# Four small moves in the order of work of an attention-then-experts kernel on one core

## The chip, the cores and the metric

The kernel runs on one core of a Trainium2 chip. Its time is the device time in microseconds (us), the median of several runs. The engines of the core are named as in the profile: PE (TensorE matmul) and PEld (its weight loads), DVE (VectorE), ACT (ScalarE), POOL (GpSimd) and SP (SyncE, which here only issues DMAs). Matmuls and weight loads are in float32 for all that matters here; the trace shows each such matmul as two passes, so 4 matmuls are "x8".

## The reference, cut to what matters

Two blocks follow each other. The first is an attention without softmax, the second routes each row by a hash to one of eight experts.

```python
def _attn_ref(q, k, v, S1, S2):          # q, k, v: (4, 4, 1088, 32); S1, S2: (8, 32)
    def phi(x):                          # 64 features of a row
        a = np.einsum('rd,bhsd->bhsr', S1, x)
        b = np.einsum('rd,bhsd->bhsr', S2, x)
        return np.einsum('bhsi,bhsj->bhsij', a, b).reshape(*x.shape[:-1], r * r)
    q_p, k_p = (phi(q), phi(k))
    kv = np.einsum('bhsf,bhsd->bhfd', k_p, v)
    ...                                  # num = q_p @ kv, den = q_p @ sum(k_p)
    return (num / den).astype(np.float32)

def _moe_ref(x, token_ids, w1, w2):      # x: (4352, 128), w1: (8, 128, 1024), w2: (8, 1024, 128)
    expert_idx = token_ids * np.int64(2654435761) % np.int64(E)
    for e in range(E):
        xe = x[mask]                     # rows of expert e
        out[mask] = np.maximum(xe @ w1[e], 0.0) @ w2[e]
```

## The kernel before, in words

**Order.** The whole kernel stands in a hand-written schedule: every engine runs its instructions in the order in which the Python code records them. So where a line stands in the code decides what is queued behind it on its engine. Waits between engines are semaphores that a tile framework puts in, by regions of tiles.

**Loads.** SP issues all input loads at the start (L95 to L152), in this order: k of batch 0 in two halves, k of batch 1, q of batch 0 in two halves, v of batch 0 in two halves, then the tails (the last 64 of a batch's 1088 rows: two DMAs for k, two for v), q of batch 1, two DMAs for the tails of q, v of batch 1, and then batches 2 and 3 and the first expert weights. A tail tile holds two batches in partitions 0 to 63 and two in 64 to 127, and each DMA of `load_tail` (L102, issue at L106) fills one half. Completion semaphores of these DMAs are used in turn, eight of them, so a DMA's issue waits until the one eight places ahead has landed.

**Attention, batch by batch.** For k, PE transposes the rows (L421), ACT copies them out of PSUM (L429), PE multiplies with the sketch matrices (L455, tile `ab_ps`), ACT copies the result (L470), DVE multiplies the two sketches into features `kp` (L482, 1024 columns per half of a batch), and PE sums `kv` over the batch's rows (L513). The tail's features are `kp_tail` and its `kv` matmuls come last in each batch. For q, DVE transposes 32 by 32 blocks (`q_blocks`, L549; for batch 0 written out at L683, in halves), PE multiplies (L455, `abq_ps`), ACT copies, DVE makes features `f` (L482) and transposes them to `fT` (L565), and PE multiplies them with `m`, the block-diagonal copy of `kv` that ACT makes (L535), into `x_ps` (L617). The q tails go through `q_tail_blocks` (L573), L582, `q_tail_features` (L602, L605) and `x_tail_products` (L626). ACT copies `x_ps` to `xe` (L620, L629); `denominators` (L639, L640) and `x_main` (L645) with `x_tail` (L659) divide and write rows to a DRAM tensor `x_rows` (DMAs at L653 and L661). `x_main` runs on POOL for batches 0 and 1 and on DVE for batches 2 and 3.

**Prologue around the change.** Between the loads and the loop over batches the code (L666 to L709) builds the routing of tokens (DVE L291 to L318, PE L299, POOL `route_firsts`, `route_digits`, `route_slots`) among the first features of k and q. On DVE the order is: scan of the routing, `kp` first half, q's blocks of batch 0 in two halves, four routing steps, the sum of digits, `kp` second half, `f` and `fT` of the first half of q, q's blocks of batch 1, `kp_tail`, blocks of the q tail, and `f` and `fT` of the second half.

**Experts.** 16 groups of work follow (256 columns each for the first eight, 320 for the overflow eight). Group g does eight steps c: `layer1` (L891) and, for the group before, `layer2` (L899). The results of `layer1` are evicted by ACT for even c (L765) and by DVE for odd c (L767). In group 0 there is no `layer2` yet, so its steps are half as long. Other work is hung on a step by `at(g, c, f, ...)` and runs after that step's matmuls. Gathers of rows from `x_rows` (POOL indirect DMAs, L759) go ahead of the groups that need them, each with a small DVE copy of its index (L811); the tiles of the first eight groups read only rows of batches 0 and 1. `turn_in` and `join_in` (L830, L831, L836) transpose gathered rows by DMA, `bring` (L822) by PE. `rows_of` (tag `xs`) has one buffer, so the rows of batch 3 wait until the DMA has read those of batch 2.

Of the kernel before, what the change touches and what calls it, by code (L numbers as in the profile page):

```python
# [9 lines left out]
F32 = mybir.dt.float32  # L10
# [20 lines left out]
def kernel(  # L31
# [12 lines left out]
    nc = tc.nc  # L44
    P = 128
    B, H, S, D = q.shape
# [4 lines left out]
    T = S // P  # L51
    SM = T * P
    SP = S - SM
    TT = B // 2
    Q = P // D
# [19 lines left out]
    work = ctx.enter_context(tc.tile_pool(name="work", bufs=2))  # L75
# [23 lines left out]
    def tail_rows(b):  # L99
        return slice(b // TT * SP, (b // TT + 1) * SP)  # L100

    def load_tail(src, name):  # L102

        t = const.tile([P, TT, H, D], F32, name=name)
        for b in range(0, B, TT):
            nc.sync.dma_start(t[tail_rows(b)].rearrange("p t h d -> p (t h) d"),  # L106
                              src[b:b + TT, :, SM:, :].rearrange("t h p d -> p (t h) d"))
        return t

    def load_main(src, b, tag):  # L110
        t = load.tile([P, H, T, D], F32, tag=tag, name=f"{tag}{b}")
        n = parts(b, tag)
        for g in range(n):
            nc.sync.dma_start(t[:, :, g * T // n:(g + 1) * T // n],
                              src[b, :, g * SM // n:(g + 1) * SM // n, :].rearrange("h (p t) d -> p h t d", t=T // n))
        return t
# [5 lines left out]
    k_t, v_t, q_t = [], [], []  # L122
# [23 lines left out]
    k_tail = load_tail(k, "k_tail")  # L146
    v_tail = load_tail(v, "v_tail")
    q_t.append(load_main(q, 1, "q"))
    q_tail = load_tail(q, "q_tail")
    v_t.append(load_main(v, 1, "v"))  # L150
    for b in range(2, B):
        load_batch(b)  # L152
# [53 lines left out]
    GQ = T // Q  # L206
# [89 lines left out]
    def route_counts():  # L296
        cnt = bank([P, 3, E], "cnt")
        for n, w in enumerate((before, ones_h, early)):
            nc.tensor.matmul(cnt[:, n], w[:], cp[:], start=True, stop=True)  # L299
        counts = const.tile([P, 3, E], F32, name="counts")  # L300
        nc.scalar.copy(counts[:], cnt[:])
        return counts
# [4 lines left out]
    def route_bases(cnt):  # L307
        nc.vector.tensor_scalar(took[:], cnt[:, 2], float(GE), None, op0=OP.min)
        nc.vector.tensor_tensor(left[:], cnt[:, 1], took[:], op=OP.subtract)

        base = const.tile([P, E], F32, name="base")
        nc.vector.scalar_tensor_tensor(base[:], took[:], float(1 << RB), cnt[:, 0], op0=OP.mult, op1=OP.add)
        nc.vector.tensor_tensor(seq[:], seq[:], base[:].unsqueeze(2).to_broadcast([P, E, C]), op=OP.add)
# [21 lines left out]
    def route_firsts():  # L335

        nc.gpsimd.memset(late[:], 1.0)
        nc.gpsimd.tensor_scalar(first[:], eid[:], float(GE), -1.0, op0=OP.mult, op1=OP.add)
        nc.gpsimd.tensor_scalar(first_late[:], eid[:], float(GL - GE), float(E * GE), op0=OP.mult, op1=OP.add)
# [84 lines left out]
    def transposed(src, g):  # L424
        return kT_copied(turned(src, g))
# [32 lines left out]
    def k_products(kTs):  # L458

        ab_ps = bank([P, T // Q, H, Q, 2 * R], "ab_ps")  # L460
        for g, kT in enumerate(kTs):
            for h in range(H):
                wide_products(ab_ps[:, g, h:min(h + 2, H)], kT[:, h], s_k[:])
        return ab_ps

    def ab_tile():
        return work.tile([P, T, H, 2, R], F32, tag="ab", name="ab", bufs=3)

    def copy_ab(ab, ab_ps, g, src=None):
        nc.scalar.copy(ab[:, g:g + Q].rearrange("p t h x r -> p t h (x r)"),  # L470
                       ab_ps[:, g // Q if src is None else src].rearrange("p h t y -> p t h y"))

    def copied(ab_ps):

        ab = ab_tile()
        for g in range(0, T, Q):
            copy_ab(ab, ab_ps, g)
        return ab

    def features(dst, ab, eng=nc.vector):  # L480
        shape = list(dst.shape)
        eng.tensor_tensor(dst, ab[:, :, 0].unsqueeze(3).to_broadcast(shape),  # L482
                                ab[:, :, 1].unsqueeze(2).to_broadcast(shape), op=OP.mult)
# [8 lines left out]
    def k_features_of(kp, ab, lo, hi, eng=nc.vector):  # L492
        features(kp[:, lo:hi].rearrange("p t h i j -> p (t h) i j"), ab[:, lo:hi].rearrange("p t h x r -> p (t h) x r"), eng)

    def values(vsrc, n, pool, tag, copy=nc.gpsimd.tensor_copy):

        va = pool.tile([P, n, H, DA], F32, tag="va" + tag, name="va" + tag, bufs=1)
        nc.gpsimd.memset(va[:, :, :, D:DA], 1.0)
        if copy:
            copy(va[:, :, :, 0:D], vsrc[:].rearrange("p h t d -> p t h d"))  # L500
        return va
# [41 lines left out]
            nc.scalar.copy(m[r, :, h], kv[r, :, h * DA:(h + 1) * DA])  # L543
        return m

    def q_blocks(src, n):

        qT = work.tile([P, H, n, D], F32, tag=f"qT{n}", name="qT", bufs=1)
        nc.vector.transpose(qT[:].rearrange("p h t s -> p (h t s)"), src[:].rearrange("p h t d -> p (h t d)"))  # L549
        return qT  # L550

    def q_products(qT, n):
# [17 lines left out]
    def q_tail_blocks():  # L570

        qT = work.tile([P, TT, H, FB, D], F32, tag="xs", name="qT_tail", bufs=1)
        nc.vector.transpose(qT[:].rearrange("p t h k s -> p (t h) k s"),  # L573
                            q_tail[:].rearrange("p t h d -> p (t h) d").unsqueeze(2).to_broadcast([P, TT * H, FB, D]))
        return qT
# [93 lines left out]
    route_scan()  # L669
    va = values(v_t[0], T, work, "", None)  # L670
    route_firsts()
    abk = ab_tile()
    kp = work.tile([P, T, H, R, R], F32, tag="kp", name="kp", bufs=1)
    parts_ps = [k_products(kTs[g:g + 1]) for g in range(GQ)]
    copy_ab(abk, parts_ps[0], 0, src=0)
    nc.scalar.copy(cp[:], seq[:, :, C - 1])
    copy_ab(abk, parts_ps[1], Q, src=0)
    k_features_of(kp, abk, 0, Q)
    cnt = route_counts()
    kTs = [transposed(k_t[1], g) for g in range(0, T, Q)]  # L680
    qT = work.tile([P, H, T, D], F32, tag=f"qT{T}", name="qT", bufs=1)
    for g in range(GQ):
        nc.vector.transpose(qT[:, :, g * Q:(g + 1) * Q].rearrange("p h t s -> p h (t s)"),  # L683
                            q_t[0][:, :, g * Q:(g + 1) * Q].rearrange("p h t d -> p h (t d)"))
    route_bases(cnt)
    digits = route_ranks()
    k_features_of(kp, abk, Q, T)
# [2 lines left out]
    for g in range(GQ):  # L690
        ts = slice(g * Q, (g + 1) * Q)
# [11 lines left out]
    kv = kv_products(0, (kp, va), (kp_tail, va_tails), kv, T)  # L703
    abk = copied(abk_ps)
    fTs = [q_features(abq, 0)]
    qT = q_blocks(q_t[1], T)
    k_features_of(kp_tail, abt, 0, TT)
    qT_tail = q_tail_blocks()
    fTs.append(q_features(abq, 1))  # L709

    for b in range(EB):
        kv = kv_products(b, (kp, va), (kp_tail, va_tails), None if b else kv)
        if b > 0:
            abk_ps = k_products(kTs)
        abq_ps = q_products(qT, T)
        va = values(v_t[b + 1], T, work, "")
        if b == 0:
            route_slots()
        if b == 0:
            abt_ps = q_tail_products(qT_tail)  # L720
        m = kv_diagonal(b, kv)
        if b == 0:
            tail = q_tail_copied(abt_ps)
            kT_ps = [turned(k_t[b + 2], g) for g in range(0, T, Q)]
        else:
            abk = copied(abk_ps)
        kp = k_features(abk, T, work, "")
        if b == 0:
            fT_tail = q_tail_features(tail)

        x_products(b, 0, fTs[0], m)
        abq = copied(abq_ps)
        m_tail = kv_tail(b, kv)
        x_products(b, 1, fTs[1], m)
        x_tail_products(b, m_tail)
        qT = q_blocks(q_t[b + 2], T)
        if b == 0:
            kTs = [kT_copied(p) for p in kT_ps]
            fTs = [q_features(abq, 0)]
            route_rows(0)  # L740
            route_tiles()
        else:
            route_tiles_p()
            kTs = [transposed(k_t[b + 2], g) for g in range(0, T, Q)]
            route_rows(1)
        denominators(b, 0, GQ * HQ + H)
        for g in range(GQ):
            x_main(b, g, nc.gpsimd)
        x_tail(b, nc.gpsimd)
        if b == 0:  # L750
            load_experts(range(E // 2, E - 2))
        if b == 0:
            fTs.append(q_features(abq, 1))
        else:
            fTs = [q_features(abq, 0)]
# [83 lines left out]
    b, e = EB, EB + 1  # L839
# [7 lines left out]
    abk, abq = copied(abk_ps), copied(abq_ps)  # L847
# [4 lines left out]
    kp = k_features(abk, T, work, "")  # L852
# [151 lines left out]
    def at(g, c, f, *a):  # L1004
        beside.setdefault((g, c), []).append(lambda: f(*a))
# [10 lines left out]
            at(g, 1 + c, fetch_tile, *ahead.pop(0))  # L1016
    assert not ahead

    for g, c in zip(range(GQ), (1, 4)):
        at(0, c, x_main, e, g, nc.vector)  # L1020
    at(0, 5, x_tail, e, nc.vector)
    for k in range(11, G):
        for j in range(tiles_of(k)[1]):
            at(k - 3, 1 + j, fetch_tile, k, j)
# [28 lines left out]
    g, lo = G - 1, GL - P  # L1053
# [40 lines left out]
    with tc.For_i(0, turns):  # L1094
# [19 lines left out]
        at = moe.tile([P, C], F32, tag="at", name="at", bufs=1)  # L1114
# [70 lines left out]
```

## Time and profile before

| what | value |
|---|---|
| median of 5 runs | 196.41 us (195.55 to 197.03) |
| the profiled execution's own time | 195.88 us |
| its span, first to last instruction | 194.2 us |
| mean granted TensorE clock | 0.990 |
| PE, DVE, POOL, ACT busy | 185.3, 111.3, 103.1, 73.7 us |
| DMA moved | 26.09 MB, mean 134 GB/s |

The span is 1.7 us shorter than the execution's own time. Timeline rows have the start, the length, the engine, the line, the operation, the tiles and sizes, the number of instructions merged, and in brackets how long the engine had stood idle and what ended that. The view of stages has, for each stretch of time, the busy time of every engine with its number of instructions, then the granted clock, the share of the 16 DMA engines and GB/s. PE's busy time counts modelled ends of pipelined matmuls, so short gaps between matmuls do not show in it; they are found from the starts.

### The profile page before, as it was taken

How to read it: one execution, taken by the hardware profiler on the slowest of the kernel's cores; microseconds unless marked ns; L12 is line 12 of the kernel's file. 1: busy time of each engine (PE TensorE's matmuls, PEld its weight loads, DVE VectorE, ACT ScalarE, POOL GpSimd, SP SyncE). 2: the span in 40 equal slices, each digit the busy share in tenths (PEclk: the TensorE clock that was granted, in tenths of full speed). 3: DMA queues.
4: the chain of work that ended last, by engine and by line, in shares of the span. 5: the costliest groups of instructions: out<-in, count | busy, mean ns of one | idle time of the engine just before them, and what ended most of it. 6: DMA issues, size and time to landing. Idle time of an engine off the chain costs nothing. (4 is left out here: it accounts for less than half of the span.)

```text
span 194.2 us, 3346 instructions
## 1 busy us (share of the span) xinstructions
PE 185.3 (95%) x1064; PEld 155.7 (80%) x1064; DVE 111.3 (57%) x302; ACT 73.7 (38%) x227; POOL 103.1 (53%) x137
## 2 busy tenths in 40 slices
PE   7989999999999999999999999999999999999960
PEld 2889999999998888888888887777777777777960
DVE  5699999999968843454345344253446625232320
ACT  6552874758365323322332322223313231321220
POOL 7228982818464466466655744656465441434650
PEclk9999999999999999999999999999999999999995
DMA  4969999999379452333324324222243421300100
GB/s 130 292 128 271 351 359 340 341 363 334 102 192 316 138 125 68 71 81 80 85 67 102 79 68 93 56 68 71 68 93 65 92 70 27 66 14 25 48 27 9
DMA packets 40737, 26.09 MB, mean 134 GB/s; under 512 B 21785, under 2 KB 37916, under 8 KB 40720
## 3 DMA queue, kind: packets, MB, share of 16 engines
q1 hardware_dynamic: 35888, 19.15, 35.4%
q0 software_dynamic: 2304, 4.59, 8.9%
q10 hardware_dynamic: 2528, 2.13, 3.8%
q8 instruction: 9, 0.15, 0.3%
q14 instruction: 8, 0.07, 0.1%
HBM read 17.47 MB, written 4.59 MB: 114 GB/s over the span
## 5 line engine op out<-in xcount | busy, mean ns | idle before, releaser
L891 PE MATMUL hp<-xT,w 128*128 128x256 f32 (+3 forms) x272 | 81.8, 393 | 0.0
L899 PE MATMUL op<-hT,w 128*128 128x256 f32 (+2 forms) x256 | 79.0, 399 | 0.0
L767 DVE TENSOR_SCALAR hT<-hp 128x256 f32<-128x256 f32 (+3 forms) x68 | 29.8, 440 | 64.3 <-PE hp L891 61.4
L891 PEld LDWEIGHTS hp<-xT,w 128*128 128x128 f32 x272 | 50.1, 190 | 11.7 <-DVE hT L767 0.4
L902 POOL DMA_INDIRECT out_dram<-os,put x36 | 36.1, 1003 | 43.2 <-DVE os L955 27.6
L899 PEld LDWEIGHTS op<-hT,w 128*128 128x128 f32 x256 | 48.2, 190 | 12.8
L765 ACT ACTIVATE hT<-hp 128x256 f32<-128x256 f32 (+3 forms) x68 | 27.2, 400 | 66.9 <-PE hp L891 66.9
L759 POOL DMA_INDIRECT xg<-x_rows,idx x34 | 35.0, 1029 | 20.5 <-DVE idx L811 8.1
L617 PE MATMUL x_ps<-m,fT 128*128 128x132 f32 x128 | 15.7, 279 | 0.1
L513 PE MATMUL kv<-va,kp 128*128 128x132 f32 x128 | 15.6, 278 | 0.0
L617 PEld LDWEIGHTS x_ps<-m,fT 128*128 128x128 f32 x128 | 14.9, 190 | 0.4 <-ACT xe L620 0.3
L513 PEld LDWEIGHTS kv<-va,kp 128*128 128x128 f32 x128 | 14.9, 190 | 0.1
L934 ACT COPY half<-op 128x256 uint16<-128x256 uint16 (+1 forms) x26 | 8.8, 392 | 13.2 <-PE op L899 13.2
L535 ACT COPY m<-kv 32x66 f32<-32x66 f32 x48 | 9.9, 206 | 7.3 <-PE kv L513 6.7
L482 DVE TENSOR_TENSOR kp<-ab 128x1024 f32<-128x1024 f32 x8 | 11.1, 1414 | 0.8 <-ACT ab L470 0.8
L482 DVE TENSOR_TENSOR f<-ab 128x1024 f32<-128x1024 f32 x8 | 10.5, 1311 | 0.1
L565 DVE STREAM_TRANSPOSE fT<-f 128x1024 f32<-128x1024 f32 x8 | 10.0, 1246 | 0.5
L645 POOL TENSOR_TENSOR xs<-xe,den 128x512 f32<-128x512 f32 x4 | 4.9, 1243 | 8.6 <-DVE f L482 5.1
L455 PE MATMUL abq_ps<-s_k,qT 128*128 128x128 f32 (+1 forms) x64 | 7.8, 275 | 0.6 <-DVE qT L683 0.6
L455 PEld LDWEIGHTS abq_ps<-s_k,qT 128*128 128x128 f32 x64 | 7.5, 192 | 0.8 <-ACT kT L429 0.8
L830 DVE COPY xh<-xg 128x256 uint16<-128x256 uint16 (+1 forms) x28 | 8.1, 330 | 0.0
L455 PE MATMUL ab_ps<-s_k,kT 128*128 128x128 f32 (+1 forms) x64 | 7.7, 274 | 0.0
(171 smaller groups left out, 155.5 us busy)
## 6 DMA issues: line engine op xcount, KB each, us to landing
w<-in_moe_w_dram SPq DMA_DIRECT2D x12, 512.0 KB, 7.8
w<-in_moe_w_dram ACTq DMA_DIRECT2D x4, 512.0 KB
k<-in_k_dram SPq DMA_DIRECT2D x3, 512.0 KB, 7.8
q<-in_q_dram SPq DMA_DIRECT2D x3, 512.0 KB
v<-in_v_dram SPq DMA_DIRECT2D x3, 512.0 KB, 7.6
x_rows<-xs SPq DMA_DIRECT2D x3, 512.0 KB, 2.8
out_dram<-os,put POOLq DMA_INDIRECT x36, 2.3
xg<-x_rows,idx POOLq DMA_INDIRECT x34, 2.8
```

The costliest lines, as they stand in the source:

```text
L455: nc.tensor.matmul(dst, stationary, s.rearrange("p t x r -> p t (x r)").unsqueeze(1).to_broadcast([s.shape[0], n, s.shape[1], 2 * R]), sta ...
L482: eng.tensor_tensor(dst, ab[:, :, 0].unsqueeze(3).to_broadcast(shape), ab[:, :, 1].unsqueeze(2).to_broadcast(shape), op=OP.mult)
L513: nc.tensor.matmul(kv[:].rearrange("p x y -> p (x y)")[:, pr * HA:(pr + 1) * HA], kp[:, t, 2 * pr:2 * pr + 2].rearrange("p h i j -> p (h i ...
L535: copy(m[f][t * D:(t + 1) * D, h::2, t], src)
L565: nc.vector.transpose(fT[:].rearrange("p k (q s) -> p k q s", q=Q), f[:].rearrange("p q h (k d) -> p (h k) q d", d=D))
L617: nc.tensor.matmul(p[:, h], fT[:, (h0 + h) * FB + fb], m[fb][:, h0 + h].rearrange("p t d -> p (t d)"), start=(fb == 0), stop=(fb == FB - 1 ...
L759: nc.gpsimd.indirect_dma_start(out=dst, out_offset=None, in_=x_dram[0:rows], in_offset=bass.IndirectOffsetOnAxis(ap=idx, axis=0), bounds_c ...
L765: nc.scalar.activation(dst, src, AF.Relu if relu else AF.Copy)
L767: return nc.vector.tensor_scalar(dst, src, 0.0, None, op0=OP.max).ins
L891: nc.tensor.matmul(hp[:, 0:hi - lo], w1[:, g % E, c * P:(c + 1) * P], x_columns(first_of(g) + lo, first_of(g) + hi), start=True, stop=True)
L899: nc.tensor.matmul(ops[g][:, 0:hi - lo], w2[:, g % E, c], hTs[g][:, c, lo:hi], start=(c == 0), stop=(c == FC - 1))
L902: st_ = nc.gpsimd.indirect_dma_start(out=out[:], out_offset=bass.IndirectOffsetOnAxis(ap=idx, axis=0), in_=src, in_offset=None, bounds_che ...
```

## The change

Four edits. (1) The rows of batch 3 (`x_main` and `x_tail` with e = 3, on DVE) are hung on steps 1, 3 and 6 of group 1 and no longer on steps 1, 4 and 5 of group 0. (2) In the prologue, q's two half transposes of batch 0 stand ahead of the first half of `kp`. (3) q's blocks of batch 1 are made in two halves, and behind `kp_tail` where they stood ahead of it. (4) The second DMA of the q tail is issued by POOL, behind `route_firsts`, and no longer by SP behind the first.

On the engines this gives: PE and ACT keep their order; DVE has one instruction more; POOL has one DMA more, ahead of its copies of the v tail; SP has one DMA less ahead of v of batch 1, and the two row writes of batch 3 stand one behind each of the first two transposing DMAs of the experts' stage, where before they stood ahead of both.

```diff
-    def load_tail(src, name):
+    def load_tail_part(t, src, b, eng):
+        eng.dma_start(t[tail_rows(b)].rearrange("p t h d -> p (t h) d"),
+                      src[b:b + TT, :, SM:, :].rearrange("t h p d -> p (t h) d"))
+
+    def load_tail(src, name, n=B):
...
-        for b in range(0, B, TT):
-            nc.sync.dma_start(t[tail_rows(b)].rearrange("p t h d -> p (t h) d"),
-                              src[b:b + TT, :, SM:, :].rearrange("t h p d -> p (t h) d"))
+        for b in range(0, n, TT):
+            load_tail_part(t, src, b, nc.sync)
...
-    q_tail = load_tail(q, "q_tail")
+    q_tail = load_tail(q, "q_tail", TT)
...
-    def q_blocks(src, n):
+    def q_blocks(src, n=1):
 
-        qT = work.tile([P, H, n, D], F32, tag=f"qT{n}", name="qT", bufs=1)
-        nc.vector.transpose(qT[:].rearrange("p h t s -> p (h t s)"), src[:].rearrange("p h t d -> p (h t d)"))
+        qT = work.tile([P, H, T, D], F32, tag="qT", name="qT", bufs=1)
+        for g in range(n):
+            ts = slice(g * T // n, (g + 1) * T // n)
+            nc.vector.transpose(qT[:, :, ts].rearrange("p h t s -> p h (t s)"), src[:, :, ts].rearrange("p h t d -> p h (t d)"))
...
     route_firsts()
+    load_tail_part(q_tail, q, TT, nc.gpsimd)
...
-    k_features_of(kp, abk, 0, Q)
     cnt = route_counts()
     kTs = [transposed(k_t[1], g) for g in range(0, T, Q)]
-    qT = work.tile([P, H, T, D], F32, tag=f"qT{T}", name="qT", bufs=1)
-    for g in range(GQ):
-        nc.vector.transpose(qT[:, :, g * Q:(g + 1) * Q].rearrange("p h t s -> p h (t s)"),
-                            q_t[0][:, :, g * Q:(g + 1) * Q].rearrange("p h t d -> p h (t d)"))
+    qT = q_blocks(q_t[0], GQ)
+    k_features_of(kp, abk, 0, Q)
     route_bases(cnt)
...
     fTs = [q_features(abq, 0)]
-    qT = q_blocks(q_t[1], T)
     k_features_of(kp_tail, abt, 0, TT)
+    qT = q_blocks(q_t[1], GQ)
     qT_tail = q_tail_blocks()
...
-    for g, c in zip(range(GQ), (1, 4)):
-        at(0, c, x_main, e, g, nc.vector)
-    at(0, 5, x_tail, e, nc.vector)
+    for g, c in zip(range(GQ), (1, 3)):
+        at(1, c, x_main, e, g, nc.vector)
+    at(1, 6, x_tail, e, nc.vector)
```

More of the change, by code (lines that the diff above doesn't have):

```diff
@@ L735 @@
         x_tail_products(b, m_tail)
-        qT = q_blocks(q_t[b + 2], T)
+        qT = q_blocks(q_t[b + 2])
         if b == 0:
```

## The prediction

> **What bounds the kernel now.** I read the page's busy times first, then the view of stages, then the timeline around the four edits. The share of busy time and the stages say that PE leads from 20 us on:
>
> ```profile
> PE 185.3 (95%) x1064; PEld 155.7 (80%) x1064; DVE 111.3 (57%) x302; ACT 73.7 (38%) x227; POOL 103.1 (53%) x137
> ```
>
> ```profile
> 5.00:10.00 5.00, 4.54 (x37) 3.90 (x35) 3.31 (x8) 2.84 (x8) 1.04 (x7) 1.00 1.04 293
> 10.00:15.00 5.00, 4.45 (x40) 4.42 (x40) 4.66 (x10) 2.58 (x6) 1.65 (x2) 1.00 0.66 143
> 15.00:20.00 5.00, 4.77 (x43) 4.61 (x42) 4.97 (x6) 1.50 (x6) 4.42 (x9) 1.00 0.95 265
> 20.00:25.00 5.00, 5.00 (x47) 5.00 (x47) 4.80 (x5) 4.36 (x22) 4.76 (x7) 1.00 1.09 359
> ```
>
> The second thing to see is DVE (third busy time): 57% of the span, but 4.66 to 4.97 of every 5 us from 10 us on, and so on to 50 us. The page's average hides that DVE has no room in the very stage in which the change moves its work. The timeline has the places where PE stands still, and what DVE does there:
>
> ```profile
> 8.03 1.23 DVE L482 TENSOR_TENSOR kp<-ab 128x1024 f32<-128x1024 f32 x1 [0.58 <-ACT ab L470]
> 9.00 1.06 PE L421 MATMUL kT_ps<-ident,k 128*128 128x128 f32 x8 [0.46 <-DMA k<-in_k_dram]
> 9.76 0.71 DVE L683 STREAM_TRANSPOSE qT<-q 128x512 f32<-128x512 f32 x1 [0.50 <-DMA q<-in_q_dram]
> 10.62 2.00 PE L455 MATMUL abq_ps<-s_k,qT 128*128 128x128 f32 x16 [0.55 <-DVE qT L683]
> 10.68 0.71 DVE L683 STREAM_TRANSPOSE qT<-q 128x512 f32<-128x512 f32 x1 [0.21 <-DMA q<-in_q_dram]
> ...
> 18.15 0.65 DVE L482 TENSOR_TENSOR kp_tail<-ab 128x512 f32<-128x512 f32 x1
> 18.95 0.69 PE L513 MATMUL kv<-va_tail,kp_tail 128*128 128x132 f32 x4 [0.23 <-DVE kp_tail L482]
> ...
> 25.07 0.71 DVE L605 STREAM_TRANSPOSE fT_tail<-f 128x512 f32<-128x512 f32 x1
> 26.68 0.45 PE L626 MATMUL x_ps<-m_tail,fT_tail 128*64 128x66 f32 x4
> ...
> 48.53 2.35 DVE L482 TENSOR_TENSOR kp<-ab 128x1024 f32<-128x1024 f32 x2
> 50.41 3.76 PE L513 MATMUL kv<-va,kp 128*128 128x132 f32 x32
> ...
> 64.14 0.69 DVE L645 TENSOR_TENSOR xs<-xe,den 128x512 f32<-128x512 f32 x1 [0.66 <-DMA x_rows<-xs]
> 64.81 0.42 DVE L767 TENSOR_SCALAR hT<-hp 128x256 f32<-128x256 f32 x1
> 65.28 0.73 PEld L891 LDWEIGHTS hp<-xT,w 128*128 128x128 f32 x4 [0.40 <-DVE hT L767]
> ```
>
> Three stalls of PE can be won. At 10.62 PE waits for q's first blocks: its eight passes from 9.00 take 8 x 0.11 = 0.88, so it could have gone on at 9.88 and loses 0.74. At 18.95 it waits for `kp_tail`. Its four matmuls from 17.60 (x8) end at 8 x 0.113 = 0.90, at 18.50, so 0.45 is lost. At 65 us ten passes of 0.216 from 63.82 should have ended at 65.98, and `layer2` began at 66.25: 0.27 lost. Together 1.46 us, 0.7% of 195.88. No edit touches anything else that PE waits for.
>
> **Edit 1, batch 3's rows in group 1.** The reader sees DVE idle for 0.66 at 64.14, waiting for the DMA that reads batch 2's rows. Behind this `xs` stands the eviction of 64.81, and PE waits for that. Moved to group 1 the wait is gone (that DMA landed by 64.1), and group 0's DVE work is 4 evictions x 0.42, one `xT` copy of 0.41, two index copies of 0.15 and two `xh` copies (0.50): 2.9 us in 8 x 0.43 = 3.45. So 0.27 comes back. In group 1 a step lasts 0.86 (the evictions of odd steps are 1.72 apart), and the added 0.69 + 0.68 + 0.29 fit: worst are steps 3 and 4 with 0.42 + 0.15 + 0.68 + 0.15 + 0.58 = 1.98, 0.26 over. That makes the eviction of step 5 late by 0.26, while PE needs its bank only four steps later (3.4 us). The rows' landing moves from 68.9 to some 74; the first gather that can read them is issued in group 4, after 87 us. On SP the two row writes (0.32 and 0.45 to issue) go in front of the transpose of 70.11, whose result DVE takes at 78.0. **-0.27.**
>
> **Edit 2, q ahead of `kp`.** The row of 9.76 decides: DVE stood idle for 0.50 and was released by q's DMA, not by its own work; so for the second half, by 0.21. `kp` (1.23) had filled the time before the landing. Put behind q's blocks it fills nothing: the blocks still start at 9.76 and 10.68, PE still starts at 10.62, and everything on DVE from the routing steps on comes later by one step of `kp`, 1.13 (13.28 to 14.41, from one such operation's start to the next). **No gain at 10.62, DVE 1.13 late.** `kp` itself is wanted at 14.23 and would end at 12.6; the digits wait for POOL until 16.17.
>
> **Edit 3, halves behind `kp_tail`.** Unshifted, `kp_tail` could start at 18.07, when ACT's copy of its input ends (17.80 + 0.27), instead of 18.15. Shifted, DVE reaches it at 18.16 (17.03 + 1.13): the same time as before. So the stall at 18.95 stays; the edit only saves it from growing by 1.1. Two halves cost 2 x 0.62 from start to start instead of 1.12, so DVE is 1.25 late behind them. The first half ends at 19.45; with the 0.15 that lies between DVE's end and PE's start at 18.95, PE's start at 19.48 becomes 19.6: 0.1.
>
> **Who pays for a late DVE.** Behind the prologue I looked for the PE instruction with the least room. `fT_tail` ends at 25.78 and PE uses it at 26.68. DVE waited 0.16 for ACT ahead of it (24.35), so its lateness is 1.09 there: 26.87, plus 0.15 is 27.02, 0.35 late (it takes in the 0.1). At 35.33 DVE waited 0.19 for ACT, which leaves 0.9. At 48.53 the first half of `kp` ends at 49.71; 0.9 and 0.15 more is 50.76, and PE, 0.35 late itself, comes at 50.76. Just no more is lost. At 54.96 DVE waits 1.57 for `kv`, and its lateness ends. **+0.35**, without the cover of those two waits +0.70 (1.25 less 0.55 of room at 50.41).
>
> **Edit 4, the q tail by POOL.** SP saves an issue (0.63), so v of batch 1 and all behind it are issued 0.6 earlier; after 10.68 no wait of PE or DVE on a load is listed, so this gains nothing. POOL's issue: its indirect DMAs take 1.0 to 1.96, SP's tail issues 0.6 to 2.0; POOL was idle 7.07 us until 13.29, so even four of its 1.0 are hidden. What is not hidden is the traffic. The DMA now starts near 6.3, when the queue is full (111.6% of 16 engines from 6 to 10 us) and q's halves are landing (issue 3.41, 7.2 us to landing: 10.65). From 10.8 to 12.8, where only tails moved, 865 packets took 37.2% of 16 x 2 us, 13.8 ns each; 512 packets over 16 engines are 0.44 us. If they come behind q's, they cost 0; if they are served among them, q and everything that hangs on it is 0.44 later; a gain is excluded, as nothing of q's is behind the DMA that leaves SP. I take 0.3: POOL's nearest row lands 2.8 after its issue, about 9.1, before q's halves.
>
> Here a rule weighs against the edit. The Trainium skill, "DMA: Bandwidth & Descriptors", section "Queues, rings and completion order", says that a DMA engine takes turns between its queues, a whole packet at a time. By it the full 0.44 would be paid and the sum would be 0.14 higher; first come, first served would make it 0.3 lower. No row before has two busy queues at once at this place, so the trace doesn't tell.
>
> **Sum.** -0.27 + 0.35 + 0.3 = +0.38. Against the profiled execution: 195.88 + 0.38 = 196.26 (span 194.2, 1.7 around it). That execution is 0.53 under the median of the runs shown; from the median, 196.41 + 0.38 = **196.8**.
>
> **Rivals.**
> - *A, the forecast:* 196.8, own range 196.1 to 197.4; chance 0.48.
> - *B, slower: DVE's lateness reaches PE in full.* Place: `kv` of batch 3 at 50.41, the tightest after the prologue. Price: 0.70 as above, 0.44 of traffic, and one collision of DVE with POOL's reads, of which the row of `f` at 44.40 shows one (1.94 where others take 1.22, 0.72), counted half, 0.36; less 0.27: +1.2, 197.6. It decides from a lateness of 0.9 at 48.5 on. For it: DVE's 4.8 of 5 us. Against: PE's own lateness gives DVE room. Chance 0.24.
> - *C, faster: q lands earlier than in this profile.* If q's first half is there by 8.0, when DVE is free (its scan ends at 7.45), the 0.74 at 10.62 goes, `kp` follows in time and DVE isn't late; with 0.27 of edit 1 and a quarter of the 0.45 at 18.95: -1.1, 195.3. Against: the row of 9.76. For: landings can differ between runs, and runs spread over 1.5 us. Chance 0.14.
> - *D, the late DVE and the traffic cost nothing, or edits 2 and 4 move nothing that is seen:* -0.27, 196.1. Chance 0.14.
>
> **Numbers.** A measurement of this kernel can tell about 0.5%, 0.98 us, from no change. Faster by that: most of C, 0.13. Slower: most of B, 0.23. The rest, A, D and edges, 0.64. The range goes from C's price to just beyond B's, 195.4 to 197.7.
>
> **What would show it.** Right: at q's blocks DVE still has an idle time ended by q's DMA, longer than 0.50; `kp` follows them; the first `abq_ps` not before 10.6; a bracket of PE ahead of L626 for `fT_tail`; none at `hp` in group 0. Wrong: `abq_ps` right behind `kT_ps`, which is C; a bracket of PE at `kv` of batch 3, which is B; q landing where it did, which takes 0.3 off.

## The result and the profile after

The changed kernel takes 195.49 us (median of 52 runs, 194.28 to 197.92), the kernel before in the same session 195.94 (94 runs). The ratio is 0.9973, 95% interval 0.9963 to 0.9983: 0.27% or about 0.5 us faster. Ratios leave out executions far above a kernel's fastest, so they can differ a little from the ratio of two medians. The forecast was 0.38 slower; the time lies in the range, the sign was wrong. Of the 1.31 us between 196.8 and 195.49, 0.47 is the base (five runs gave 196.41, 94 gave 195.94), 0.38 the sum itself and 0.45 the gain that came in its place.

The profiled execution of the changed kernel took 195.81 (span 194.1), beside 195.88 (194.2) before. These two say nothing of a gain; it took many runs to see it. From the page after, the busy times:

```profile
PE 185.7 (96%) x1064; PEld 156.2 (80%) x1064; DVE 112.1 (58%) x303; ACT 74.0 (38%) x227; POOL 103.8 (53%) x138
```

DVE has its one instruction more, POOL its one DMA. The timeline after at the first products (start, length, engine, line; the lines of the unchanged code are 3 to 5 higher than before):

```profile
6.23 0.95 POOL L103 DMA_DIRECT2D q_tail<-in_q_dram  x1
...
8.89 1.07 PE L424 MATMUL kT_ps<-ident,k 128*128 128x128 f32 x8
...
9.16 0.71 DVE L554 STREAM_TRANSPOSE qT<-q 128x512 f32<-128x512 f32 x1 [1.72 <-DMA q<-in_q_dram]
...
10.02 1.69 PE L458 MATMUL abq_ps<-s_k,qT 128*128 128x128 f32 x13
10.04 0.71 DVE L554 STREAM_TRANSPOSE qT<-q 128x512 f32<-128x512 f32 x1 [0.17 <-DMA q<-in_q_dram]
10.67 1.18 DVE L485 TENSOR_TENSOR kp<-ab 128x1024 f32<-128x1024 f32 x1
```

DVE now idles 1.72 for q's DMA, where before `kp` filled the time, and `kp` follows q's blocks. Everything here is 0.60 earlier than before (first `abq_ps` 10.02, not 10.62), because q's first half landed at 9.13 and not at 9.73, and not because DVE takes q first: the distance from landing to `abq_ps` is 0.89 in both. The same timeline where the late DVE should reach PE, PE alone:

```profile
22.41 1.06 PE L424 MATMUL kT_ps<-ident,k 128*128 128x128 f32 x8 [0.68 <-DMA k<-in_k_dram]
23.31 3.77 PE L622 MATMUL x_ps<-m,fT 128*128 128x132 f32 x32
27.02 0.45 PE L631 MATMUL x_ps<-m_tail,fT_tail 128*64 128x66 f32 x4
```

The expected bracket for `fT_tail` at 27.02 is missing: PE had just lost 0.68 to the load of k of batch 2, so it came late itself. (This place, where PE multiplies `m_tail` with `fT_tail`, L626 before and L631 after, is called the q tail's product below.) And DVE in group 0 of the experts:

```profile
63.36 0.42 DVE L770 TENSOR_SCALAR hT<-hp 128x256 f32<-128x256 f32 x1 [0.19 <-PE hp L894]
63.70 0.20 DVE L814 COPY idx<-get 128x1 int32<-128x1 int32 x2
64.16 0.42 DVE L770 TENSOR_SCALAR hT<-hp 128x256 f32<-128x256 f32 x1 [0.26 <-PE hp L894]
...
67.81 0.68 DVE L650 TENSOR_TENSOR xs<-xe,den 128x512 f32<-128x512 f32 x1
```

Here edit 1 does what it should: between two evictions no idle time ends in a DMA of `x_rows`, and the rows stand at 67.81, in group 1, with no wait of PE. From group 0's first product to the first `layer2` it takes 66.34 - 62.13 = 4.21, where before it took 4.48.

### The profile page after: what moved, and what is told of

Its sections match the earlier page's. It is cut to its first block, busy times and chain, and to the rows that moved or that the text cites. A ratio compares the mean times of both kernels' runs of the same rounds, so it can differ in the third digit from the quotient of the medians.

```text
span 194.1 us, 3348 instructions
## 1 busy us (share of the span) xinstructions
PE 185.7 (96%) x1064; PEld 156.2 (80%) x1064; DVE 112.1 (58%) x303; ACT 74.0 (38%) x227; POOL 103.8 (53%) x138
## 5 line engine op out<-in xcount | busy, mean ns | idle before, releaser
L458 PEld LDWEIGHTS ab_ps<-s_k,kT 128*128 128x128 f32 x64 | 7.6, 193 | 0.1
```

The costliest lines, as they stand in the source:

```text
L458: nc.tensor.matmul(dst, stationary, s.rearrange("p t x r -> p t (x r)").unsqueeze(1).to_broadcast([s.shape[0], n, s.shape[1], 2 * R]), sta ...
```

## The experiments

Each kernel below ran 12 times beside 23 to 35 runs of the kernel before on the same chip (its median there is given). Ratios are against those, with a 95% interval. Edits are numbered as in the change.

### Parts alone

Four kernels with whole hunks of the change: edit 1 alone; edits 2 and 3; edit 4 alone; edits 1, 2 and 3. Before: 196.14.

```diff
 # e1_rows_group1: in the kernel before
-    for g, c in zip(range(GQ), (1, 4)):
-        at(0, c, x_main, e, g, nc.vector)
-    at(0, 5, x_tail, e, nc.vector)
+    for g, c in zip(range(GQ), (1, 3)):
+        at(1, c, x_main, e, g, nc.vector)
+    at(1, 6, x_tail, e, nc.vector)
 # e2_e3_q_first: in the kernel before, q_blocks as in the change, and
-    k_features_of(kp, abk, 0, Q)
...
+    qT = q_blocks(q_t[0], GQ)
+    k_features_of(kp, abk, 0, Q)
...
-    qT = q_blocks(q_t[1], T)
     k_features_of(kp_tail, abt, 0, TT)
+    qT = q_blocks(q_t[1], GQ)
 # e4_tail_by_pool: in the kernel before, load_tail as in the change, and
-    q_tail = load_tail(q, "q_tail")
+    q_tail = load_tail(q, "q_tail", TT)
...
+    load_tail_part(q_tail, q, TT, nc.gpsimd)
 # e1_e2_e3_no_pool: the first two together
```

> Edit 1 alone. Theory now (the gain is edit 1's, and the late DVE is paid for by nobody, because behind the prologue PE waits for the load of k of batch 2): 0.27 us faster than before, about 0.14%, with no wait of PE in group 0 of the experts. Rival 1 (the gain is q's earlier start, edit 1 only moves a wait): no change, and a new wait in group 1.

Measured: 195.65, 0.9981 (0.9957 to 1.0005). 4.21 in group 0, as in the changed kernel.

> Edits 2 and 3 alone. Theory now: within 0.2 us of before; where q lands late (9.7) nothing is won at the first q products, where it lands early PE starts them up to 0.7 earlier and gives that back at the load of k of batch 2. Rival 1: 0.3 to 0.5 us faster, all of the change's gain. The prediction on record had 0.35 slower.

Measured: 196.12, 1.0007 (0.9977 to 1.0036). Its timeline has the forecast bracket; PE alone:

```profile
25.34 1.06 PE L622 MATMUL x_ps<-m,fT 128*128 128x132 f32 x8
26.72 0.42 PE L631 MATMUL x_ps<-m_tail,fT_tail 128*64 128x66 f32 x4 [0.32 <-DVE fT_tail L610]
```

> Edit 4 alone. Theory now: 0 to 0.2 us faster, since the changed kernel's q tail reached the DMA engines only at 9 us, behind q's halves, and the loads behind it are issued 0.6 earlier. The prediction on record had 0.3 slower, by q's halves landing later. Rival 2 (edit 4 carries the gain, by an earlier landing of k of batch 2): 0.4 faster, k of batch 2 landing 0.4 earlier.

Measured: 196.06, 0.9997 (0.997 to 1.0024). q's first half landed at 9.08; no loss of 0.3.

> The change without edit 4. Theory now: 0.3 us faster than before, like edit 1 alone. Rival 2 (edit 4 carries the gain): as before. Rival 1: 0.5 faster, as the whole change.

Measured: 195.87, 0.9991 (0.9967 to 1.0015), with a bracket of 0.26 for `fT_tail`. None of the four intervals leaves out 1, so these runs alone decide nothing. In the traces edit 1 brings group 0 to 4.21, edits 2 and 3 bring the bracket, and edit 4 costs nothing that can be seen.

### One part undone

The changed kernel without edits 2 and 3; without edit 1; without edit 2; and once more as it is. Before: 197.33 (another chip).

```diff
 # e1_e4_old_order: the lines of e2_e3_q_first taken back in the changed kernel
 # e2_e3_e4_old_rows: those of e1_rows_group1 taken back
 # e1_e3_e4_k_first: edit 2 alone taken back
+    k_features_of(kp, abk, 0, Q)
     cnt = route_counts()
     kTs = [transposed(k_t[1], g) for g in range(0, T, Q)]
     qT = q_blocks(q_t[0], GQ)
-    k_features_of(kp, abk, 0, Q)
```

> The change without edits 2 and 3 (DVE's order in the prologue as before). Theory (edit 1 gives 0.27, edits 2 and 3 only make DVE late, which costs 0.4 at the q tail's product where nothing else holds PE up): 0.3 us faster than before and 0 to 0.4 faster than the changed kernel; no wait of PE for the q tail's transposed features. Rival (edits 2 and 3 give what is over 0.27): 0.2 slower than the changed kernel.

Measured: 196.46, 0.9967 (0.9941 to 0.9993).

> The change without edit 1. Theory: 0.27 slower than the changed kernel, PE losing 0.27 to 0.36 in group 0 as before. Rival (the gain is in the prologue): as the changed kernel.

Measured: 197.22, 0.9989 (0.9959 to 1.0019). Without edit 1 group 0 takes 4.50 again.

> The changed kernel with edit 2 undone: k's first features ahead of q's blocks again. Theory: PE starts the first q products 0.9 after q's first half has landed, as in every run so far; DVE is not late, no wait at the q tail's product; 0 to 0.4 us faster than the changed kernel. Rival C (q lands early outside profiles, so edit 2 wins up to 0.7): 0.3 or more slower than the changed kernel.

Measured: 196.47, 0.9953 (0.9926 to 0.998).

> The changed kernel once more, for a second profile and a comparison on this chip: 0.2 to 0.5 us faster than before. Theory: where k of batch 2 lands by 21.6 there is no wait of 0.8 at its transposes, and then PE waits 0.4 for the q tail's transposed features instead; where that load lands late, as in the first profile, the wait is there and the other is not.

Measured: 196.72, 0.9973 (0.995 to 0.9996). In this profile k of batch 2 landed at 19.88, and the bracket at the q tail's product is 0.11, not the 0.4 expected. The kernel with edit 2 undone looked 0.4 better than the changed one; the next group didn't confirm it.

In the ten profiles so far q's first half landed at 8.55 to 9.13 with edit 4 and at 9.25 to 9.73 without. I took that for the cause of a gain and tested it.

### Is it the DMA by POOL?

All four on one chip, before 197.47.

```diff
 # e1_e3_k_first_no_pool: edits 2 and 4 undone in the changed kernel (edit 2 as above)
-    q_tail = load_tail(q, "q_tail", TT)
+    q_tail = load_tail(q, "q_tail")
...
-    load_tail_part(q_tail, q, TT, nc.gpsimd)
 # e1_e3_e4_pool_issue_late: edit 2 undone, and POOL's issue recorded later
-    load_tail_part(q_tail, q, TT, nc.gpsimd)
...
     digits = route_ranks()
+    load_tail_part(q_tail, q, TT, nc.gpsimd)
```

> The changed kernel with edits 2 and 4 undone (edits 1 and 3 stay). My theory of edit 4: its 0.26 (pooled from four pairs of runs so far) is real and comes in the prologue, so this kernel is 0.26 slower than the one with edits 1, 3 and 4; in the profile q's first half lands later than 9.2 (profiles without edit 4 so far: 9.25 to 9.73, with it 8.55 to 9.13). Rival: the landing is decided by slow packets of k of batch 1 between 4.4 and 6.2, before the edited DMA is issued, so the earlier landings were chance: q may land anywhere from 8.5 to 9.8 here, and this kernel equals the one with edits 1, 3 and 4 within 0.1.

Measured: 196.54, 0.9959 (0.9931 to 0.9986), and q's first half landed at 8.74, without edit 4. My theory fell: an early landing doesn't need edit 4. The delay is there already in k of batch 1, which is ahead of q on the queue (in the first profile of before 15 of its 16 parts landed by 7.32 and the last at 8.86; q follows 0.87 behind), and in every profile of this and the earlier groups k landed before POOL's DMA had sent a packet. Why one or two parts come late I can't tell.

> Edits 1, 3 and 4 (k's features ahead of q's blocks), but POOL issues the q tail's second half behind its digits, near 16 instead of 6.2; SP issues the same DMAs as in the changed kernel. Theory that the early DMA by POOL is what matters: q lands late again (9.2 to 9.8) and the kernel is 0.26 slower than the next. Theory that the freed 0.6 of SP matters (v of batch 1 and k of batch 2 issued earlier): it is as fast as the next, within 0.1. Theory that edit 4 does nothing: all three of this call's k-first kernels are within 0.1 of each other. The risk of its own is a wait of DVE at the q tail's blocks (24 us) if the tail lands later than that: not expected, POOL's DMA took 6.3 to land, which gives 22.5.

Measured: 196.46, 0.9951 (0.9923 to 0.9979). This experiment doesn't do what it was made for: POOL records nothing between the two places, so its issue stayed at 6.25. In their profiles this kernel and the next have the same instructions in the same order on every engine, and so the two tell how far like kernels come apart.

> The changed kernel with edit 2 undone, once more. It was 0.9953 of the time before, the changed kernel on the same chip 0.9973. My theory: edit 2 only makes DVE 1.1 late and costs 0.2 to 0.4 at the q tail's product, so this one is 0.2 to 0.4 faster than the changed kernel again, 0.995 to 0.996 of before; in the profile no wait of PE for fT_tail beyond 0.10. Rival: the 0.4 was chance of that call, and both are at 0.997.

Measured: 196.86, 0.9965 (0.994 to 0.999). The profile misses what was expected of it: without edit 2 there is a bracket of 0.46 at the q tail's product.

```profile
26.83 0.42 PE L631 MATMUL x_ps<-m_tail,fT_tail 128*64 128x66 f32 x4 [0.46 <-ACT xe L625]
```

It names ACT, but `fT_tail` ended at 26.68, and 0.15 from DVE's end to PE's start is what the other waits at this place have (26.57 to 26.72 in the kernel with edits 2 and 3 alone). What made DVE late here is taken up below.

> The changed kernel once more, as the partner of the other three on the same chip: 0.9965 to 0.998 of before. If edit 2 costs what I think, 0.2 to 0.4 slower than the kernel with edits 1, 3 and 4; if the rival that edit 2 wins outside of the profiles holds (q landing by 8.0 in most executions), it is 0.3 or more faster than that kernel.

Measured: 196.86, 0.9958 (0.9928 to 0.9987). Its profile has a full wait at the q tail's product:

```profile
25.32 0.84 PE L622 MATMUL x_ps<-m,fT 128*128 128x132 f32 x6
26.80 0.42 PE L631 MATMUL x_ps<-m_tail,fT_tail 128*64 128x66 f32 x4 [0.65 <-DVE fT_tail L610]
```

Yet its runs are as fast as those of the three kernels without edit 2 (0.9951 to 0.9965): edit 2's loss isn't confirmed, my claim of 0.2 to 0.4 isn't either, and two like kernels differ by 0.0014.

### The two prices by themselves

One chip, before 197.43. Both new kernels are made from the changed one. The open question was whether the prices of a late DVE (0.35) and of the traffic (0.3) are wrong, or their places.

> The kernel before against itself: the ratio tells what two equal kernels differ by, 0.999 to 1.001. Its second profile tells what was chance in the first: if q's landing is set by slow packets and not by edit 4, its first half can land below 9.2 here (9.73 in the first profile); from the first product of the experts' group 0 to the first of the second layer it takes 4.48 again, 0.27 or more over the 4.21 of the kernels with edit 1.

Measured: 197.46, 0.9983 (0.9954 to 1.0011): two equal kernels differ by 0.0017, more than the 0.001 that was expected. The kernel before again: 4.50 in group 0, and q's first half landed at 8.70, without any edit.

> Edit 1 alone once more. The runs so far, fitted together, give it 0.48 less (0.29 to 0.67), the traces 0.27 to 0.37. My theory: it is 0.27 to 0.5, 0.9975 to 0.9985, and the three other edits are within 0.2 of nothing. Rival: edit 1 alone is no more than its 0.27 and the rest of the changed kernel's gain comes from edit 4; then this is 0.9986 or above.

Measured: 196.51, 0.9952 (0.9925 to 0.998); 4.21 in group 0. The rival (0.9986 or above) lies outside this interval; the first run of the same kernel, 0.9981 (0.9957 to 1.0005), doesn't exclude it.

```diff
 # q_tail_ahead_of_q
     k_t += [load_main(k, b, "k") for b in range(2)]
+    q_tail = const.tile([P, TT, H, D], F32, name="q_tail")
+    load_tail_part(q_tail, q, TT, nc.sync)
     q_t.append(load_main(q, 0, "q"))
...
-    q_tail = load_tail(q, "q_tail", TT)
+    load_tail_part(q_tail, q, 0, nc.sync)
...
-    load_tail_part(q_tail, q, TT, nc.gpsimd)
 # dve_one_more_kp
     k_features_of(kp, abk, 0, Q)
+    k_features_of(kp, abk, 0, Q)
```

> The changed kernel with the second part of q's tail issued by SP ahead of q of batch 0, not by POOL. It tests the price that I gave to edit 4, at the place where I thought its packets would be. Theory that the price is right and only the place was wrong (POOL's packets start at 9.3, behind q's first half): q's first half lands some 0.44 later here than k of batch 1 does in other runs (0.87 to 0.91 behind it; here 1.3), and the time is 0.3 to 0.5 over the changed kernel's, 0.999 to 1.0 of before. Rival, that a load of 512 packets is hidden wherever it goes: the changed kernel's 0.997.

Measured: 196.85, 0.9971 (0.9943 to 0.9998). The distance from the landing of k of batch 1 to that of q's first half is a steady measure: 0.86 to 0.92 in eighteen profiles, those of all kernels but this and the next. Here it is 9.94 - 8.76 = 1.18. So the same 64 KB ahead of q, 512 packets on SP's queue, cost it 0.28, not 0.44. In the time this doesn't show, but 0.28 us is 0.0014, about half of the interval's half-width. Each theory is half right.

> The changed kernel, with the first half of k's features computed twice behind q's blocks: DVE is later by a further 1.13 (a step of kp). It tests what a late DVE costs. Theory of the prediction (0.35 of 1.09 lateness reaches PE at the q tail's product, with no room left behind it): all of the further 1.1 is paid, the wait at that product is 1.2 to 1.5 in the profile and the time 0.9 to 1.2 over the changed kernel's, 1.001 to 1.003 of before. Rival, that DVE has more room in most executions than the profile of before shows (loads that land late hold PE anyway): 0.5 or less over the changed kernel's, 0.9995 or below.

Measured: 197.64, 0.998 (0.9947 to 1.0013), the slowest kernel with edit 1. Its timeline (the third row is PE at `kv` of `kp`'s second half, the fourth at `kv` of the tail; a bracket counts from the modelled end of the matmul ahead):

```profile
10.06 1.54 DVE L554 STREAM_TRANSPOSE qT<-q 128x512 f32<-128x512 f32 x2 [2.64 <-DMA q<-in_q_dram]
...
11.53 2.44 DVE L485 TENSOR_TENSOR kp<-ab 128x1024 f32<-128x1024 f32 x2
...
17.69 1.14 PE L516 MATMUL kv<-va,kp 128*128 128x132 f32 x8 [0.94 <-DVE kp L485]
...
20.69 0.58 PE L516 MATMUL kv<-va_tail,kp_tail 128*128 128x132 f32 x3 [0.52 <-DVE kp_tail L485]
```

A late DVE does cost in this execution: from start to start PE lost 1.10 at the first place, where the other kernels lose nothing, and 0.68 at the second (about 0.4 in the other kernels), so some 1.4 more than they, over the 1.13 that was added. But it is paid in the prologue, not at the q tail's product, where nothing is lost (0.22 from start to start, as in the kernel before). The time lies, by the ratios, 0.1 to 0.3% or 0.2 to 0.6 us over those of the other kernels of this group and the last with edit 1. That is nearer to the rival, 0.5 or less, than to the theory, 0.9 to 1.2. The trace's 1.4 lies over both; the profiled execution, 198.53, was the slowest of the twelve, so it doesn't stand for the others.

By chance this run shows edit 4's price too. The packets of POOL's queue are q0 in the view of the DMA queues; from 6 to 9 us, first the changed kernel, then this one:

```profile
q1 hardware_dynamic: 1741, 0.93, 112.6%
```

```profile
q1 hardware_dynamic: 1657, 0.89, 107.2%
q0 software_dynamic: 19, 0.05, 5.9%
```

In nine of ten profiles with edit 4 POOL's packets begin between 9.23 and 9.55, 2.4 to 3.3 us behind the issue, when q's first half has landed or all but landed, and the distance is 0.88 to 0.92. Here they began at 8.35, and it is 10.04 - 8.90 = 1.14: 0.24 more.

### How much of edit 1 is the one wait?

Both are made from the kernel with edit 1 alone. Before: 197.19.

```diff
 # e1_half_of_rows                      # e1_rows_group2: at(2, ...) in all three
-    for g, c in zip(range(GQ), (1, 3)):
-        at(1, c, x_main, e, g, nc.vector)
+    for g, c in zip(range(GQ), (1, 1)):
+        at(g, c, x_main, e, g, nc.vector)
     at(1, 6, x_tail, e, nc.vector)
```

> Edit 1 by halves: the first half of batch 3's rows stays in group 0 (at step 1), the second half, whose multiplication waited for the DMA of batch 2's rows, and the tail go to group 1. If the one wait for that DMA is all of edit 1's gain, 4.48 between the first product of group 0 and the first of the second layer becomes 4.21 as in edit 1, or a little over it (DVE's work in group 0 is 2.9 + 0.69 = 3.6 beside 3.45 of PE), and the time is edit 1's, 0.995 to 0.998 of before. If the rows' transfers or DVE's load in group 0 are what edit 1 takes away, half of the gain goes: 0.998 to 1.0, with 4.3 to 4.5 in the trace.

Measured: 197.24, 1.0007 (0.998 to 1.0033). I had the halves wrong: it is the first that waits for the buffer, so this kernel keeps the wait and moves all that could stay. DVE in group 0, and PE:

```profile
64.26 0.69 DVE L650 TENSOR_TENSOR xs<-xe,den 128x512 f32<-128x512 f32 x1 [1.10 <-DMA x_rows<-xs]
```

```profile
65.40 1.13 PE L893 MATMUL hp<-xT,w 128*128 128x256 f32 x4 [0.44 <-DVE hT L769]
```

Group 0 takes 4.92. With the wait kept, nothing of edit 1's gain is left in the trace, though half of the rows and the tail have left the group. The runs say it less clearly: 1.0007 isn't told from the 0.9989 of the next kernel, which has the whole of edit 1's 4.21. And the wait isn't always as long: the DMA of batch 2's rows was issued 0.53 ahead of group 0's first product here and 0.54 in the profile of before, and DVE got past it 2.81 and 2.37 behind that product. This execution lost 0.71 to it, those of the four kernels without edit 1 0.27 to 0.37.

> Edit 1, but with the rows in group 2 in place of group 1. If the one wait in group 0 is all, the same as edit 1 alone: 0.995 to 0.998 of before and 4.21 in the trace. If there is more to win than the traces show because the rows still crowd group 1, it is faster than 0.995; if the first gather that reads these rows then waits (it is issued after 87, the rows would land near 78), slower than 0.998, with an idle time of POOL or PE behind 87.

Measured: 196.98, 0.9989 (0.9966 to 1.0013), 4.21 in group 0. The ratio is over the 0.995 to 0.998 expected, within its interval. Group 1 wasn't crowded: nothing more is won. Behind 93.1 PE lost 0.38 that the other kernels don't have, and I didn't find what held the eviction there.

## Why the prediction was wrong

All runs of the session can be read at once: each time is fitted by least squares as the chip's level in that group plus a price for each edit (450 runs: the kernel before, the changed kernel, and all but the four kernels with an edit of their own). The intervals hold only the scatter of the runs. With the kernel that has the rows in group 2 counted as edit 1, edit 1's price is -0.49 ± 0.15.

| step | predicted | in the traces | fitted to the runs |
|---|---|---|---|
| edit 1 | -0.27 | -0.27 to -0.37 | -0.53 ± 0.17 |
| edits 2 and 3, the late DVE | +0.35 | 0.17 to 0.71 over the usual at the q tail's product in four profiles, up to 0.03 in three; 0.52 in one without edit 2 | +0.11 ± 0.18 |
| edit 4, traffic | +0.3 | 0 in nine profiles, 0.24 on q's landing in one | -0.14 ± 0.18 |

**The step that failed is edit 4's: "I take 0.3: POOL's nearest row lands 2.8 after its issue, about 9.1, before q's halves".** That row was of an indirect DMA. The real one sends its first packet 3.0 after the issue (6.23 to 9.27) and lands at 12.36. So its packets come behind q's first half. The price itself was too high as well: the prediction counted 512 packets, but on POOL's queue the same 64 KB are 32, 16 of them over 2 KB. In the kernel with edit 4 alone, from 9.3 to 12:

```profile
DMA packets 1873, 0.45 MB, mean 167 GB/s; under 512 B 1449, under 2 KB 1857, under 8 KB 1873
q0 software_dynamic: 32, 0.07, 9.0%
```

9.0% of 2.7 us on each of the 16 engines is 0.24, and 0.24 is what the one execution paid in which they came among q's. "A gain is excluded" holds in the traces; in the runs, 0.14 ± 0.18 is not told from nothing. The same section named the Trainium skill, "DMA: Bandwidth & Descriptors", section "Queues, rings and completion order", by whose turns between queues the full 0.44, the prediction's estimate, was due: where both queues were busy at q's place, 0.24 was paid, all of the price that the row above gives, and in the other nine profiles the case didn't arise.

This step doesn't turn the sign by itself: with edit 4 at nothing the sum is still +0.08. The two terms below failed too.

**Edit 2's "No gain at 10.62" held in half of the executions seen.** It was right in the profiles of before and after: `abq_ps` starts 0.89 behind q's landing in both. What the one profile couldn't say is that the order of `kp` and q's landing changes between executions. In the second profile of the kernel before:

```profile
7.36 3.06 PE L455 MATMUL ab_ps<-s_k,kT 128*128 128x128 f32 x16
...
9.61 1.23 DVE L482 TENSOR_TENSOR kp<-ab 128x1024 f32<-128x1024 f32 x1 [2.01 <-ACT ab L470]
...
10.75 1.30 DVE L683 STREAM_TRANSPOSE qT<-q 128x512 f32<-128x512 f32 x2
...
11.60 0.80 PE L455 MATMUL abq_ps<-s_k,qT 128*128 128x128 f32 x5 [0.20 <-DVE qT L683]
```

Here q was there at 8.70, and its blocks waited for `kp` until 10.75: rival C's condition, with another cause (a late `kp`). With `kp` ahead, q was there before `kp` was done in six of twelve profiles: in these `abq_ps` starts 1.03 to 2.90 behind q's landing, in the other six 0.88. With q ahead it starts 0.88 behind in seven of eight profiles, and 2.37 in the one where PE itself was late. So in six of the twelve q's blocks ahead of `kp` could have started the first products earlier, by 0.15 to 0.66 in five of them, and the prediction put this at nothing. That this is why edits 2 and 3 come out near nothing is argued from these profiles.

**Edit 3's 0.35** names the right place and the wrong cause. From start to start PE's first pass at the q tail's product comes 0.10 to 0.13 over the usual spacing in fifteen of twenty profiles. In the other five it is 0.27 (the changed kernel's second profile), 0.42 and 0.48 (the brackets of 0.26 and 0.32), 0.81 (0.65) and 0.62 (0.46, without edit 2). In the last four DVE's multiplication `f`, ahead of `fT_tail`, took 1.53 to 1.92, where alone it takes 1.18, and POOL was copying `va` when it began. In the third profile of the changed kernel:

```profile
19.64 1.04 POOL L503 COPY va<-v 128x1024 f32<-128x1024 f32 x1
19.84 1.92 DVE L485 TENSOR_TENSOR f<-ab 128x1024 f32<-128x1024 f32 x1
```

In all eight profiles in which `f` began during POOL's copy and was stretched (1.24 to 2.02), it ends 1.08 behind the end of the copy, as if DVE's work on `f` began only when the copy was done. In these four the excess (0.35, 0.41, 0.74, 0.55) is the wait over the usual 0.10 (0.32, 0.38, 0.71, 0.52) to within 0.03, so without the copy there would have been no more than the usual wait. Both are needed: in the three kernels with edit 3 whose `f` took 1.18 or 1.19 while PE was on time nothing is lost here, and with `f` at 1.69 and 2.02 but no late DVE (the second profile of before, `e1_e4_old_order`) nothing either. So the late DVE used up the room, and what was paid is a collision of DVE with POOL, which the prediction priced in rival B alone. No run moves POOL's copy by itself.

Undoing edit 2 alone doesn't take the lateness away: DVE then idles 1.00 to 1.29 ahead of `kp_tail`, and behind it edit 3 makes it as late as in the changed kernel. In the changed kernel's first profile `f` took 1.90, but k of batch 2 landed at 22.28 and hid it, and I had costed that load's 0.6 earlier issue at nothing without asking how its landing varies (19.7 to 22.4 over the profiles). The stall at `kp_tail` stayed, as said, 0.4 to 0.5 in all but two profiles (by the starts it is 0.39 in the profile of before, not 0.45). Rival B's place is false: no profile has a wait at `kv` of batch 3.

**Edit 1** was right in each instance: 4.48 to 4.21, no wait in group 1. Its size is 0.27 to 0.37 by the traces and 0.36 to 0.70 by the runs, so the prediction's 0.27 was too small. The test with the wait kept has a trace in which nothing is gained and the wait cost 0.71. That longer waits in other executions make up the difference fits this, but one row doesn't show how often, and so half of the gain's size stays open.

So the sign was wrong because a gain of 0.27, sure but priced too low, was set against two losses that one profile made look sure. Term by term, as fitted, the runs took 0.44 off edit 4, 0.24 off edits 2 and 3 and 0.26 off edit 1. No version that I tried is clearly faster than the changed kernel: its ratios are 0.9958 to 0.9973, those of the others with edit 1 in its place 0.9951 to 0.9991.

## What to carry to other kernels

A wait that is removed by moving work behind what releases it can be told from one profile, by the gap that it left on the bound engine; its size may differ between executions (0.27 in the first profile here, 0.53 ± 0.17 in the runs). A loss or a gain that depends on which of two events comes first can't, if they move between executions by more than its size: measure distances within a run (q's landing behind k's, 0.86 to 0.92) and not times from the start, which moved by 1.5 us. A DMA's traffic is to be priced where its packets come, not where it is issued, and by a row of the same kind of DMA. And where an instruction takes longer than its like (`f`, 1.92 for 1.18), look at what the engine beside it was doing before pricing the wait behind it.

## What the runs showed of the hardware

PE's full rate begins at a time that differs from run to run, and the column of the granted clock doesn't show it. The row of 7.36 above has 16 passes in 3.06, 0.21 apart until 9.7; in the changed kernel's profile the same 16 took 1.90, 0.11 apart. PE had been at work from 0.97 in both. The view of stages of the second profile of before has 7 instructions of PE in a stretch of 1 us in which it is always busy, where nine passes of 0.11 fit:

```profile
8.00:9.00 1.00, 1.00 (x7) 1.00 (x6) 0.00 (x0) 0.00 (x0) 0.00 (x0) 1.00 1.17 301
```

The column third from the end, the granted clock, reads 1.00. Over the profiles the full rate came between 4.6 and 10.3 (in three, passes are 0.11 apart from 4.7 on); the two latest have their first `abq_ps` at 11.49 and 11.60, all others at 9.43 to 10.92. This, with q's landing (8.55 to 10.04), moves the start by more than all that the four edits were about. The Trainium skill, "TensorE: Matmul & The Clock Gate", section "What's actually happening", gives about 3.4 us of sustained work until the full rate and says that it varies between runs; here it took 3.6 to 9.3 from PE's start, with stretches of up to 0.5 in which PE waited.
